# An attention kernel with a gated MLP: the first batch's maxima on the upper halves of float32 words, three weight blocks at the head of the load queue

## The chip, the cores and the metric

The kernel runs on one core of a Trainium2 chip. The metric is the time of one execution on the device in microseconds (us), as the median of several runs. The engines of the core work side by side, each through a list of its own: TensorE (PE, matrix products; its weight loads are shown as PEld), VectorE (DVE), ScalarE (ACT), GpSimd (POOL) and SyncE (SP), which here only issues DMAs.

## The reference, cut to what matters

Eight batches with eight heads of causal attention with a decay go into a two-layer MLP whose gate is `h * tanh(softplus(h))`. q, k and v are float32 with 576 rows of 64 per head; the MLP has 512 inputs, 2,048 hidden values and 512 outputs for 4,608 tokens.

```python
scores = scale * np.matmul(q, k.transpose(0, 1, 3, 2))
cum = np.cumsum(np.log(np.clip(f, 0.0001, 1.0)), axis=-1)
scores = np.where(causal, -1000000000.0, scores + cum[:, :, :, None] - cum[:, :, None, :])
scores = scores - np.max(scores, axis=-1, keepdims=True)
attn = np.exp(scores)
attn = attn / (np.sum(attn, axis=-1, keepdims=True) + 1e-09)
x = np.matmul(attn, v)            # all heads of a token side by side: 4608 x 512
h = x @ w_in
out = (h * np.tanh(np.log1p(np.exp(h)))) @ w_out
```

A row's maximum is only subtracted ahead of the exponential, and the division by the sum of the exponentials takes it out again. So it need not be exact.

## The kernel before

Two heads are worked on together as a pair, four pairs to a batch, 32 in all. Pairs 0 to 3 (the first batch, `g < NB`) go another way than the rest. A first pass, `max_items` (L1161), multiplies q with k on TensorE in float32, adds a row of decay sums (`rk`) and the causal mask, and VectorE reduces each block to row maxima (`mx`). The maxima are turned on TensorE (`mpad`, `mr`), and a second pass, `st_items`, makes the scores again, in float32 and transposed, with the maxima inside the product, so that their exponentials (`pt`) can go straight into the product with v. The maxima pass has diagonal blocks (`diag`, four of 128 columns for each of two heads), three wider ones (`t31` with 384 and 128, `t2` with 256 columns) and the last 64 rows of both heads on the full array (`t4a` with 512 columns, `t4b` with 64). Two heads' products of 64 rows run side by side in the two halves of the array.

Weights come in 32 blocks of 128 x 512 float32 values, as 64-bit words. `load_weights` (L882) brings one block by DMA; `convert_weights` (L888) makes from it, in three VectorE operations, words that ScalarE squares and sums (`junk<-wall`, into `wsq`); `scale_weights` adds the sums over the partitions on TensorE (`wsc<-wsq`, then `b<-wsc,ones`) and makes a factor from them; `split_weights` stores the scaled block as an upper half in f16 (VectorE or ScalarE) and the remainder in f16 (VectorE, `wall<-wall,wsc`). The first half of the blocks have places of their own; a later block goes to a place that a conversion has left.

`decay` (L782) makes the decay sums on VectorE and ScalarE and writes them to DRAM in two DMAs (`cumd`); `prep_first` reads rows of them back (`rk`). The write of the first head group carries the mark `rows0`. An operation with a gate counts as a reader of that mark, so it is put behind that write: all weight loads have the gate, and so have v's first loads.

The order of the work is not written out. A `Program` records all operations with their dependencies and ranks, and a planner (`schedule`, `forward`) sorts them into one list for each engine, by a model of their durations; some operations may go to either of two engines. Where the model sees TensorE idle in the first 140 us, it puts in fillers, products of `idm` and `idh` that nothing reads. An engine takes its list strictly in order. So a small edit moves rows far from itself.

In the program's lists, `qk_0`, `qk_1`, `hl` and part of `xa` are the four places that pairs 0 to 3 of q and k are loaded to, in this order; `b_0` with a number is a PSUM bank; `st_1` and `st_0` hold the decay sums while they are made.

Of the kernel before, what the change touches and what calls it, by code (L numbers as in the profile page):

```python
# [14 lines left out]
BF16 = mybir.dt.bfloat16  # L15
# [15 lines left out]
NP = 4  # L31
CH = 512
NF = 16
# [54 lines left out]
OFS = 0  # L88
KL0 = 100
KLS = 50  # L90
KS0 = 600
KSS = 50
KE0 = 900
# [7 lines left out]
NB = 4  # L101
# [580 lines left out]
def attn_moe(ctx: ExitStack, tc: tile.TileContext, qk, v, f, w_in, w_out, out):  # L682
# [99 lines left out]
    def decay():  # L782
        _, on, cm, r1 = tmp
        nc.vector.memset(on, 1.0)
        nc.vector.tensor_scalar(out=ft, in0=ft, scalar1=1e-4, scalar2=1.0, op0=ALU.max, op1=ALU.min)
        nc.scalar.activation(out=ft, in_=ft, func=AF.Ln)
        nc.scalar.preload_act_table_set("exp_and_others")
        nc.vector.tensor_tensor_scan(
            out=cm, data0=on, data1=ft, initial=0.0, op0=ALU.mult, op1=ALU.add)
        c = flat(ST2[1])[:, 0 : 3 * S].rearrange("p (r s) -> p r s", r=3)  # L790
        nc.vector.tensor_scalar(out=c[:, 0], in0=cm, scalar1=-8.0, scalar2=None, op0=ALU.mult)
        nc.vector.scalar_tensor_tensor(
            out=r1, in0=cm, scalar=-8.0, in1=c[:, 0], op0=ALU.mult, op1=ALU.subtract)
        nc.vector.tensor_copy(out=c[:, 1], in_=r1)
        nc.vector.tensor_tensor(out=c[:, 2], in0=r1, in1=c[:, 1], op=ALU.subtract)
        nc.mark = "sums"
        for h in (slice(0, H), slice(H, BH)):
            nc.mark = None if h.start else "sums"
            nc.sync.dma_start(out=cumd[h], in_=c[h])
        nc.mark = None  # L800
# [20 lines left out]
    def square_sum(o, x, scale=1.0):  # L821
        junk = sp.tile([P, S], BF16, name="junk", tag="junk", bufs=1)
        nc.scalar.activation(
            out=junk[:, 0 : free(x)] if len(x.shape) == 2 else junk.rearrange("p (n d) -> p n d", d=D),
            in_=x, func=AF.Square, scale=scale, accum_out=o)
# [41 lines left out]
    def step(x, j):  # L867
        return j + x * W1
# [12 lines left out]

    def load_weights(i):  # L882
        which, j = worder[i]
        nc.gate = 'rows0'
        nc.sync.dma_start(out=home[i], in_=(w_in, w_out)[which][:, j])
        nc.gate = None

    def convert_weights(i):  # L888

        x, j = worder[i]  # L890
        w = wall[:, i + 1].bitcast(F32)
        r, o = home[i], w.bitcast(I32)
        nc.vector.tensor_scalar(
            out=o, in0=r[:, 1::2], scalar1=3, scalar2=0x3FFFFFF8,
            op0=ALU.logical_shift_left, op1=ALU.bitwise_and)
        nc.vector.scalar_tensor_tensor(
            out=o, in0=r[:, 1::2], scalar=-(1 << 30), in1=o, op0=ALU.bitwise_and, op1=ALU.bitwise_or)
        nc.vector.scalar_tensor_tensor(
            out=o, in0=r[:, 0::2], scalar=29, in1=o, op0=ALU.logical_shift_right, op1=ALU.bitwise_or)
        square_sum(wsq[:, step(x, j), x : x + 1], w)  # L900

    def scale_weights(t0, t1):
# [146 lines left out]
        nbank += 1  # L1049
        return psum(nbank % 4)  # L1050

    def load_qk(g):
        b, p = divmod(g, NP)
        if g == 2:
            t = sp.tile([P, 2, S], F32, name=f"qk{g}", tag="hl", bufs=NHL)
        elif g == 3:
            t = xa[1].rearrange("p a h n -> p (a h n)").bitcast(F32)[:, 0 : 2 * S]
            t = t.rearrange("p (t s) -> p t s", t=2)
        else:
            t = sp.tile([P, 2, S], F32, name=f"qk{g}", tag="qk32", bufs=NQK)  # L1060
        nc.sync.dma_start(out=t, in_=qk[b, p])
        st[g]["qk"] = t

    def place1(g):
        return (g - NB) % 2

    def qz(g):
        return spare1[:, g * P : (g + 1) * P]
# [91 lines left out]

    def max_items(g):  # L1161

        x, k, z, s = st[g]["qk"], rk[:, g], qz(g), st[g]

        def begin():

# [563 lines left out]
    def gated_by(gate, f):  # L1730
        nc.gate = gate
        f()
        nc.gate = None
# [10 lines left out]
        out=psum(RB)[:, 0:DN], lhsT=idh, rhs=idm.unsqueeze(1).to_broadcast([P, DN // P, P]), start=True, stop=True))]  # L1744
    NG = B * NP
    nc.sync.dma_start(out=ft, in_=f)
    load_qk(0)
    decay()
    load_qk(1)
    for g in (2, 3):  # L1750
        gated_by('rows0', lambda: load_qk(g))

    A = []
    marks = {}
# [2 lines left out]
    def a0(fn, g=NG):  # L1757
        A.extend(leading(g, [(fn, 0)]))
# [4 lines left out]
    def slot(t, what=("max", "st", "pv")):  # L1763

        groups = []
        ahead = "max" in what and t < NG
        if ahead:
            groups.append(leading(t, max_items(t)) if t < NB else [])
        if "st" in what and 0 <= t - 1 < NG:
            groups.append(leading(t - 1, (st_items if t - 1 < NB else new_st_items)(t - 1)))  # L1770
        if "pv" in what and 0 <= t - 2 < NG:
            groups.append(leading(t - 2, (pv_items if t - 2 < NB else new_pv_items)(t - 2) + x_items(t - 2)))
        if ahead:
            b, p = divmod(t, NP)
            b1 = (t - 9 + NV) // NP
            if t == NP * b1 + 9 - NV and b1 < B - 1:
                a0(lambda: amax_v(b1 + 1))
            if t == 0 or t == EX:
                a0(lambda: prep(t), t)
                a0(lambda: prep2(t), t)  # L1780
        if ahead and t == LV0:
            a0(lambda: gated_by('rows0', lambda: load_v(0)), 0)
            a0(lambda: amax_v(0), 0)
            a0(lambda: scale_chunk2(0))
        if "st" in what and 0 <= t - 1 < NG:
            a0(lambda: prep_v(t - 1), t - 1)
            b, p = divmod(t - 1, NP)
            if p == 7 - NV and b + 1 < B:
                a0(lambda: gated_by('rows2' if b == 0 else None, lambda: load_v(b + 1)))
        merged = sorted(  # L1790
            ((k + 0.5) / len(x) * (0.75 if ahead and gi == 0 else 1.0), gi, k)
            for gi, x in enumerate(groups) for k in range(len(x)))
        half_done = not ahead
        for fr, gi, k in merged:
            A.append(groups[gi][k] + ((t, gi, k),))
            if not half_done and fr > 0.35:
                half_done = True
                if t + 1 < NB and t + 1 != EX:
                    a0(lambda: prep(t + 1), t + 1)
                elif t >= NB:  # L1800
                    a0(lambda: prep(t))
                if 4 <= t + 2 <= NB:
                    a0(lambda: load_qk(t + 2))
                elif NB < t + 1 < NG:
                    a0(lambda: load_qk(t + 1))
        if ahead and t + 1 < NB and t + 1 != EX:
            a0(lambda: prep2(t + 1), t + 1)
        elif ahead and t >= NB:
            a0(lambda: prep2(t))
        if "pv" in what and 0 <= t - 2 < NG:  # L1810
            marks[t - 2] = len(A)
# [72 lines left out]


    first = marks[NP - 1]
    wq = [ranked([KL0 + k * KLS, 0, 0.1], lambda i=k: load_weights(i)) for k in range(NF)]
    for t0, t1 in zip([0] + TB, TB):
        now = [place[x, t - x * W1] for t in range(t0, t1) for x in range(2) if 0 <= t - x * W1 < NF]
        for i in now:  # L1890
# [93 lines left out]
```

## Time and profile before

| | us |
|---|---|
| median of 3 runs | 1023.21 |
| lowest and highest | 1021.28, 1026.99 |
| the profiled execution | 1025.73 |
| span of the profiled execution, first to last instruction | 1023.6 |

| engine | busy us | share of the span | instructions |
|---|---|---|---|
| TensorE | 989.9 | 97% | 7838 |
| VectorE | 737.2 | 72% | 2018 |
| ScalarE | 712.4 | 70% | 1350 |
| GpSimd | 16.1 | 2% | 79 |

The mean granted clock of TensorE is 0.992 of full speed. A matrix product's end is modelled, so products overlap in the records: the distance from one start to the next tells what one costs, and a busy share of 97% is not 97% of what the array could do. Nearly all instructions are recorded by one helper line (L331), so rows are told apart by the names of what they write and read: `out<-in`.

### The profile page before, as it was taken

How to read it: one execution, taken by the hardware profiler on the slowest of the kernel's cores; microseconds unless marked ns; L12 is line 12 of the kernel's file. 1: busy time of each engine (PE TensorE's matmuls, PEld its weight loads, DVE VectorE, ACT ScalarE, POOL GpSimd, SP SyncE). 2: the span in 40 equal slices, each digit the busy share in tenths (PEclk: the TensorE clock that was granted, in tenths of full speed). 3: DMA queues.
4: the chain of work that ended last, by engine and by line, in shares of the span. 5: the costliest groups of instructions: out<-in, count | busy, mean ns of one | idle time of the engine just before them, and what ended most of it. 6: DMA issues, size and time to landing. Idle time of an engine off the chain costs nothing.

```text
span 1023.6 us, 20891 instructions
## 1 busy us (share of the span) xinstructions
PE 989.9 (97%) x7838; PEld 547.7 (54%) x7838; DVE 737.2 (72%) x2018; ACT 712.4 (70%) x1350; POOL 16.1 (2%) x79
## 2 busy tenths in 40 slices
PE   5999999999999999999999999999999999999998
PEld 4687444444555555445454555454545555656664
DVE  5999899997777677666767767676777659952432
ACT  2567899979777877777777777888777664533323
POOL 4000000000000000000000000000000000000000
PEclk9899899999999999999999999999999999999999
DMA  6968856678867767686868776777666343001001
GB/s 200 377 222 210 177 131 128 134 155 181 175 137 167 173 137 156 133 177 137 158 137 189 140 154 144 146 156 136 130 134 134 68 78 73 4 1 43 1 1 42
DMA packets 265079, 137.50 MB, mean 134 GB/s; under 512 B 237522, under 2 KB 237714, under 8 KB 264978
## 3 DMA queue, kind: packets, MB, share of 16 engines
q1 hardware_dynamic: 264978, 136.17, 59.3%
q8 instruction: 61, 1.00, 0.4%
q14 instruction: 40, 0.33, 0.1%
HBM read 45.46 MB, written 9.66 MB: 54 GB/s over the span
## 4 chain that ended last, share of the span: by engine, by line
PE 66%; DVE 17%; DMA 7%; ACT 5%; issue 3%; SPq 1%; POOL 1%; ACTq 0%; DVEq 0%; POOLq 0%
PE b L331 66%; DVE wall L331 4%; DVE b L331 3%; DMA pt<-hb 2%; DMA st<-hl 2%; DVE hb L331 2%; SPq L331 1%; DMA qk<-in_qk_dram 1%; DVE hl L331 1%; DMA wall<-in_w_out_dram 1%; ACT junk L331 1%; DVE x L331 1%; DVE gl L331 1%; ACT rk L331 1%; ACT more_e L331 1%
## 5 line engine op out<-in xcount | busy, mean ns | idle before, releaser
L331 PEld LDWEIGHTS <-wall 128*128 128x128 f16 x3372 | 323.1, 98 | 360.7 <-issue 25.2
L331 PE MATMUL b<-gh,wall 128*128 128x512 f16 x1152 | 366.1, 379 | 0.3 <-DVE wsc L331 0.3
L331 PE MATMUL b<-xa,wall 128*128 128x512 f16 (+1 forms) x1602 | 346.1, 366 | 8.9 <-ACT me L331 4.4
L331 PE MATMUL b<-gl,wall 128*128 128x512 f16 x576 | 218.3, 379 | 0.0
L331 DVE SCALAR_TENSOR_TENSOR gl<-me,gsc,gh 128x512 f16<-128x512 f32 x144 | 106.6, 751 | 33.5 <-ACT gh L331 32.4
L331 ACT ACTIVATE me<-b,cinv 128x512 f32<-128x512 f32 (+1 forms) x130 | 85.2, 660 | 53.9 <-PE b L331 52.7
L331 DVE CUSTOM_DVE_ANT_0 b<-b,mskw 128x256 f32<-128x256 f32 (+2 forms) x168 | 95.3, 570 | 21.3 <-PE b L331 17.0
L331 PE MATMUL b<-st 128*128 128x384 f16 (+11 forms) x672 | 106.8, 299 | 2.6 <-ACT rk L331 1.3
L331 ACT ACT_TABLE_LOAD x76 | 97.5, 1283 | 1.3
L331 PEld LDWEIGHTS <-st 67*128 67x128 f16 (+3 forms) x864 | 68.9, 101 | 54.4 <-issue 16.9
L331 PE MATMUL b<-vv,pt 128*128 128x65 f16 (+3 forms) x2464 | 94.4, 199 | 3.5 <-DVE x L331 1.6
L331 ACT ACTIVATE more_e<-b,mn 128x512 f32<-128x512 f32 (+3 forms) x126 | 64.9, 543 | 37.5 <-DVE mn L331 33.5
L331 PEld LDWEIGHTS <-pt 128*128 128x128 f16 (+1 forms) x2352 | 72.4, 101 | 19.2 <-DMA pt<-hb 3.5
L331 ACT ACTIVATE rk<-b,mn 128x512 f32<-128x512 f32 (+3 forms) x126 | 64.4, 543 | 24.2 <-DVE mn L331 22.7
L331 DVE TENSOR_TENSOR hb<-more_e,hb 128x512 f16<-128x512 f32 x84 | 57.7, 688 | 28.3 <-ACT hb L331 27.8
L331 DVE TENSOR_TENSOR hb<-rk,hb 128x512 f16<-128x512 f32 x84 | 57.4, 688 | 22.7 <-ACT hb L331 22.4
L331 DVE TENSOR_SCALAR gh<-me,gsc 128x512 f16<-128x512 f32 x67 | 32.4, 485 | 41.6 <-ACT me L331 40.4
L331 ACT ACTIVATE hb<-more_e 128x512 f16<-128x512 f32 x84 | 51.9, 626 | 7.1 <-DMA pt<-hb 6.6
L331 ACT ACTIVATE gh<-me,gsc 128x512 f16<-128x512 f32 x77 | 54.9, 718 | 1.7
L331 DVE TENSOR_TENSOR me<-b,hb 128x256 f32<-128x256 f32 x42 | 18.0, 432 | 51.1 <-PE b L331 50.5
L331 ACT ACTIVATE hb<-rk 128x512 f16<-128x512 f32 x84 | 51.4, 625 | 4.2 <-DMA pt<-hb 2.3
L331 ACT ACTIVATE junk<-qk 128x576 bf16<-128x576 f32 x56 | 38.1, 680 | 19.7 <-DMA qk<-in_qk_dram 19.0
(189 smaller groups left out, 1078.8 us busy)
## 6 DMA issues: line engine op xcount, KB each, us to landing
st<-hl SPq DMA_DIRECT2D x168, 144.0 KB
qk<-in_qk_dram SPq DMA_DIRECT2D x30, 576.0 KB
out_dram<-ot SPq DMA_DIRECT2D x36, 256.0 KB
v<-in_v_dram SPq DMA_DIRECT2D x30, 288.0 KB
wall<-in_w_in_dram SPq DMA_DIRECT2D x16, 512.0 KB
wall<-in_w_out_dram SPq DMA_DIRECT2D x16, 512.0 KB
pt<-hb SPq DMA_TRANSPOSE x168
hl<-in_qk_dram SPq DMA_DIRECT2D x1, 576.0 KB
```

Source lines behind the costliest of these rows:

```text
L331: r = getattr(real[eng], method)(*a, **kw)
```

## The change

In `max_items` the views of q, k and the copied tail `z` become bf16 views of every second 16-bit element, which are the upper halves of the float32 words. The products there become 16-bit products, with the values cut to their upper halves; the second pass is as it was. `NUG = 3` weight blocks lose the gate `rows0`, so that their loads may go ahead of the write of the decay sums, and their conversions get a gate of their own, `parts`, which is set by the last VectorE operation of the decay sums. They are recorded right behind pair 0's load. Pairs 2 and 3 of q and k, before recorded at the head, are now recorded behind pair 0's preparation.

```diff
+NUG = 3
@@ decay
+        nc.mark = "parts"
         nc.vector.tensor_tensor(out=c[:, 2], in0=r1, in1=c[:, 1], op=ALU.subtract)
@@ load_weights
-        nc.gate = 'rows0'
+        nc.gate = 'rows0' if i >= NUG else None
         nc.sync.dma_start(out=home[i], in_=(w_in, w_out)[which][:, j])
@@ convert_weights
+        nc.gate = "parts" if i < NUG else None
         nc.vector.tensor_scalar(
...
+        nc.gate = None
         square_sum(wsq[:, step(x, j), x : x + 1], w)
@@ load_qk, now place_qk for the tile and load_qk for the DMA
+        if "qk" not in st[g]:
+            place_qk(g)
+        nc.sync.dma_start(out=st[g]["qk"], in_=qk[g // NP, g % NP])
@@ max_items
-        x, k, z, s = st[g]["qk"], rk[:, g], qz(g), st[g]
+        k, s = rk[:, g], st[g]
+        x = st[g]["qk"].bitcast(BF16)[:, :, 1::2]
+        z = qz(g).bitcast(BF16)[:, 1::2]
@@ the head of the program
+    for g in range(NB):
+        place_qk(g)
     load_qk(0)
+    for k in range(NUG):
+        load_weights(k)
     decay()
     load_qk(1)
-    for g in (2, 3):
-        gated_by('rows0', lambda: load_qk(g))
@@ slot
+        if ahead and t == 0:
+            for g in (2, 3):
+                a0(lambda g=g: gated_by('rows0', lambda: load_qk(g)), 0)
@@ the weights' queue
-    wq = [ranked([KL0 + k * KLS, 0, 0.1], lambda i=k: load_weights(i)) for k in range(NF)]
+    wq = [ranked([KL0 + k * KLS, 0, 0.1], lambda i=k: load_weights(i)) for k in range(NUG, NF)]
```

How the planner's lists change is shown at three places. The first is the head of SyncE's list. Before:

```order
L331 DMA st_1_87<-in_f_dram 64x576
L331 DMA hl_110<-in_qk_dram 128x1152
L331 DMA xa_90<-in_qk_dram 128x1152
L331 DMA qk_0_108<-in_qk_dram 128x1152
L331 DMA qk_1_109<-in_qk_dram 128x1152
L331 DMA cumd<-st_1_87 8x1728
...
L331 DMA vv_114<-in_v_dram 128x9x64
L331 DMA wall<-in_w_in_dram 128x1024 x4
L331 DMA wall<-in_w_out_dram 128x1024
```

The same place after:

```order
L332 DMA st_1_87<-in_f_dram 64x576
L332 DMA qk_0_108<-in_qk_dram 128x1152
L332 DMA wall<-in_w_in_dram 128x1024 x3
L332 DMA qk_1_109<-in_qk_dram 128x1152
L332 DMA cumd<-st_1_87 8x1728
...
L332 DMA vv_114<-in_v_dram 128x9x64
L332 DMA wall<-in_w_in_dram 128x1024
L332 DMA hl_110<-in_qk_dram 128x1152
L332 DMA wall<-in_w_out_dram 128x1024
```

Pair 0 has gone to the front with three weight blocks behind it; the loads of pairs 2 (`hl`) and 3 (`xa`, eight loads further on) have gone behind v and the fourth weight block.

The second place is VectorE's list from the last operation of the decay sums to the first reductions. Before:

```order
L331 TENSOR_TENSOR st_1_87<-st_0_86,st_1_87 64x576
L331 TENSOR_REDUCE mx_119<-b_0_124 128x1
L331 TENSOR_REDUCE mx_119<-b_0_125 128x1
L331 TENSOR_REDUCE mx_119<-b_0_120 128x4
...
L331 TENSOR_REDUCE mx_127<-b_0_124 128x4
L331 TENSOR_REDUCE am_m_117<-vc_115 128x1
L331 TENSOR_SCALAR am_m_117<-am_m_117 128x1
L331 TENSOR_SCALAR wall<-wall 128x512
```

After:

```order
L332 TENSOR_TENSOR st_1_87<-st_0_86,st_1_87 64x576
L332 TENSOR_SCALAR wall<-wall 128x512 x2
L332 SCALAR_TENSOR_TENSOR wall<-wall 128x512 x4
L332 TENSOR_SCALAR wall<-wall 128x512
...
L332 SCALAR_TENSOR_TENSOR wsc<-b_0_107,wba 128x4
L332 TENSOR_SCALAR wsc<-wsc 128x4
L332 TENSOR_SCALAR wiv<-wsc 128x4
L332 SCALAR_TENSOR_TENSOR wall<-wall,wsc 128x512
L332 TENSOR_REDUCE mx_119<-b_0_120 128x4
```

Three conversions, the scaling of two blocks and one remainder now stand between the sums and the first reduction; a second remainder stands among the reductions. `am_m<-vc`, the sum of v's squares, and the fourth block come after the reductions, as the first block did.

The third place is TensorE's list behind the first, unfinished products of pair 0. Before:

```order
L331 MATMUL b_0_122<-qk_0_108 128x384
L331 MATMUL b_0_123<-qk_0_108 128x384
L331 LDWEIGHTS idh
L331 MATMUL b_0_107<-idm,idh 128x128
...
L331 MATMUL b_0_120<-rk,xa_90 128x128
L331 LDWEIGHTS xa_90
L331 MATMUL b_0_121<-rk,xa_90 128x128
```

After:

```order
L332 LDWEIGHTS qk_0_108
L332 MATMUL b_0_123<-qk_0_108 128x384
L332 LDWEIGHTS idh
L332 MATMUL b_0_107<-idm,idh 128x128
...
L332 MATMUL b_0_107<-wsc,ones 128x4
L332 LDWEIGHTS idh
L332 MATMUL b_0_107<-idm,idh 128x128
...
L332 MATMUL b_0_120<-rk,xa_90 128x128
```

Where 34 fillers stood, there are 82 and then, behind the first column sum of weights (`wsc,ones`), 5 more. A 16-bit product has one product row and a weight load of its own. In the whole program there are 148 fillers in place of 78. The late parts of the lists are the same in both, row for row: the last 1,155 rows of VectorE's, the last 338 of SyncE's.

## Rows read from the trace of the kernel before

**Rows 1.** The page, part 4: shares of the chain of work that ended last.

```profile
PE 66%; DVE 17%; DMA 7%; ACT 5%; issue 3%; SPq 1%; POOL 1%; ACTq 0%; DVEq 0%; POOLq 0%
```

**Rows 2.** Stretches, us: busy of PE, PEld, DVE, ACT, POOL; PE's clock; DMA share; GB/s.

```profile
10.00:26.00 16.00, 11.43 (x140) 8.62 (x136) 5.52 (x15) 3.10 (x8) 2.59 (x13) 0.95 0.70 173
26.00:40.00 14.00, 12.46 (x111) 7.99 (x112) 13.33 (x40) 8.18 (x23) 0.41 (x2) 0.81 1.03 402
40.00:80.00 40.00, 39.70 (x511) 33.05 (x509) 39.61 (x105) 26.82 (x68) 0.00 (x0) 1.00 0.71 242
...
97.00:112.00 15.00, 14.96 (x73) 10.32 (x74) 12.39 (x35) 11.62 (x29) 0.14 (x1) 0.66 0.73 149
...
140.00:220.00 80.00, 78.43 (x611) 39.48 (x609) 79.36 (x237) 77.01 (x133) 0.97 (x3) 1.00 0.62 130
...
260.00:860.00 600.00, 595.08 (x4717) 303.64 (x4715) 422.11 (x1174) 451.46 (x856) 2.91 (x21) 1.00 0.68 141
```

**Rows 3.** Timeline, DVE: start, us, instruction, count, [idle before and what ended it].

```profile
8.88 0.75 DVE L331 TENSOR_TENSOR st<-st,st 64x576 f16<-64x576 f32 x1
15.40 0.76 DVE L331 TENSOR_REDUCE mx<-b 128x1 f32<-128x256 f32 x2 [5.77 <-PE b L331]
...
23.82 0.16 DVE L331 TENSOR_REDUCE am_m<-vc 128x1 f32<-128x4 f32 x1 [2.61 <-ACT junk L331]
...
25.58 0.43 DVE L331 TENSOR_SCALAR wall<-wall 128x512 int32<-128x512 int32 x1 [1.42 <-DMA wall<-in_w_in_dram]
...
31.20 0.18 DVE L331 TENSOR_SCALAR mpad<-mx 128x18 f16<-128x18 f32 x1
...
94.39 0.43 DVE L331 TENSOR_SCALAR wall<-wall 128x512 int32<-128x512 int32 x1 [1.99 <-DMA wall<-in_w_out_dram]
```

**Rows 4.** Timeline, SP's queue.

```profile
9.72 0.70 SPq L331 DMA_DIRECT2D cumd<-st  x2
...
19.65 2.63 SPq L331 DMA_DIRECT2D wall<-in_w_in_dram  x4
```

**Rows 5.** Timeline, PE's products, from 15 to 106 us.

```profile
15.03 0.34 PE L331 MATMUL b<-rk,xa 64*128 64x128 f16 x4
...
19.30 1.10 PE L331 MATMUL b<-qk,xa 128*128 128x512 f32 x2
20.24 0.38 PE L331 MATMUL b<-rk,xa 128*128 128x512 f16 x1
...
24.21 0.38 PE L331 MATMUL b<-am_m,ones 128*128 128x1 f32 x2 [3.15 <-DVE am_m L331]
26.73 2.08 PE L331 MATMUL b<-qk,xa 128*128 128x512 f32 x2 [2.13 <-DVE cols L331]
...
97.04 3.29 PE L331 MATMUL b<-vv,pt 128*128 128x65 f32 x26 [1.64 <-DVE x L331]
...
105.18 2.72 PE L331 MATMUL b<-xa,wall 128*128 128x512 f16 x6
```

**Rows 6.** Groups by form, DVE, 0 to 260 us: count | busy us, mean ns.

```profile
L331 DVE SCALAR_TENSOR_TENSOR wall<-wall 128x512 int32<-128x512 int32 x64 | 43.3, 687 | 0.2
L331 DVE SCALAR_TENSOR_TENSOR wall<-wall,wsc 128x512 f16<-128x512 f32 x32 | 23.9, 747 | 0.0
...
L331 DVE TENSOR_SCALAR wall<-wall 128x512 int32<-128x512 int32 x32 | 13.3, 423 | 3.4 <-DMA wall<-in_w_out_dram 2.0 <-DMA wall<-in_w_in_dram 1.4
```

**Rows 7.** Timeline, PE, second score pass of pair 3: 32-bit and 16-bit products.

```profile
87.46 0.81 PE L331 MATMUL b<-xa 64*128 64x384 f32 x4
88.11 0.19 PE L331 MATMUL b<-idm,msk 64*128 64x64 f16 x1
...
88.33 0.33 PE L331 MATMUL b<-xa,rk 64*128 64x384 f16 x2
88.50 0.39 PE L331 MATMUL b<-xa 64*128 64x128 f32 x4
```

**Rows 8.** The chain in order of time, one piece: start, us, what.

```profile
84.88 9.48 DMA wall<-in_w_out_dram
```

More of the change, by code (lines that the diff above doesn't have):

```diff
@@ L1050, in score_bank, with place_qk @@
         return psum(nbank % 4)
-    def load_qk(g):
-        b, p = divmod(g, NP)
+    def place_qk(g):
         if g == 2:
@@ L1060, in load_qk @@
             t = sp.tile([P, 2, S], F32, name=f"qk{g}", tag="qk32", bufs=NQK)
-        nc.sync.dma_start(out=t, in_=qk[b, p])
         st[g]["qk"] = t
+    def load_qk(g):
+        if "qk" not in st[g]:
+            place_qk(g)
+        nc.sync.dma_start(out=st[g]["qk"], in_=qk[g // NP, g % NP])
     def place1(g):
```

## The prediction

> **What bounds the kernel now.** I read the chain of work that ended last, then the table of stretches, then the timelines of VectorE, TensorE and SyncE's queue over the first 110 us. The chain is TensorE's for 66% and VectorE's for 17% [rows 1]. The table says where each has its part [rows 2]: from 260 to 860 us TensorE is busy for 595 of 600 us and VectorE for 422, so that is TensorE's stretch, and nothing there can start earlier unless what stands ahead of it does. From 140 to 220 us VectorE (79.4 of 80) and ScalarE (77.0) are full and TensorE is close behind. From 40 to 80 us TensorE (39.7) and VectorE (39.6) are full together. The only long holes are at the start: from 10 to 26 us VectorE works 5.5 us of 16, from 26 to 40 us TensorE's granted clock is 0.81 on average, and from 97 to 112 us it is 0.66.
>
> The change touches only work of the first 100 us, and the diff of the orders bears this out: the last 1,155 of VectorE's about 2,010 rows, and the last 338 of SyncE's 601, stand in the same sequence before and after. So the question is by how much the first batch (pairs 0 to 3) ends earlier, and how much of that arrives at the common tail.
>
> What holds VectorE at the start is in its timeline [rows 3]. The decay sums end at 9.63 us (8.88 + 0.75). Then it waits 5.77 us for the first finished maxima, because each score product ends with a row of the sums that has been through DRAM: SyncE sends them at 9.72 [rows 4], TensorE gets the first at 15.03 [rows 5]. It waits 2.61 us for ScalarE's squares of v and 1.42 us for the first weight block, which SyncE sends out only at 19.65, behind all of that [rows 4]. Adding the 0.5 us pieces between, 10.5 us of VectorE's time in this window are empty [rows 2].
>
> **Part 1: three weight blocks early.** A block's conversion is one shift (13.3 us for 32, 0.42 each) and two combinations (43.3 us for 64, 0.68 each), so 1.77 us [rows 6]; in a row they overlap a little, and I take 1.6. Three blocks are 4.8 us. The order shows them right behind the last operation of the decay sums, with the scaling of the first two blocks (about 0.4 us of small operations) and two of their remainders (23.9 us for 32, 0.75 each, so 1.5) ahead of or among the first reductions. That is 6.7 us of VectorE's work which before lay behind 25.6 us. It lies in the 5.77 us wait, so the first reductions, before at 15.40, start about 1.8 us later: 9.63, plus 4.8 of conversion, about 0.3 until ScalarE has squared the second block, 0.6 for the column sum on TensorE, 0.4 of scaling, 0.6 until ScalarE has the upper half, 0.75 for the remainder, is 17.1. The seven or so reductions that were spread over 15.4 to 21.2 us at TensorE's pace then run without a pause and, with the second remainder among them, end at about 22.3; the next thing, the sum of v's squares, was ready at 23.82 [rows 3]. So the delay is covered with 1.5 us to spare. The fourth block is SyncE's first weight load behind v, where the first was: it lands at about the same 25.6 us. VectorE is then 6.7 us of work ahead, and its holes from 9.6 to 25.6 us have shrunk from 10.5 to about 4.
>
> What the early loads may cost: at the head of the queue 1.5 MB of weights take the place of 1.15 MB of pairs 2 and 3, a little over 0.3 MB more. The loads of before were done by then, since nothing of SyncE's waits at 9.72; a further 0.3 MB or so at the 402 GB/s of the stretch from 26 to 40 us [rows 2] is under 1 us, and the sums are written only at 9.72. I take nothing, with 1 us as the other end. Pair 0 is first in the queue now, so its load is off the path.
>
> Pairs 2 and 3 are now loaded behind the fourth and between later blocks. Pair 2's products stand behind pair 0's second score pass, so a load sent at about 20 us has time. But blocks five to nine then stand behind 1.15 MB more, while VectorE comes to them 6.7 us sooner. At 402 GB/s [rows 2] those bytes are 2.9 us. I put the waits for blocks between 30 and 40 us at 0 to 3 us and take 1, since the common conversion pace there (1.6 us a block and other work between) is slower than a block's 1.3 us of transfer.
>
> **Part 2: maxima on 16-bit halves.** The price of a 32-bit product against a 16-bit one is in one stretch where both run on the same shapes, two heads side by side [rows 7]: 384 columns in 32 bits take from 87.46 to 88.11, 0.65 us; in 16 bits from 88.33 to 88.50, 0.17. That is 1.25 ns a column. On the full array, 512 columns in 32 bits take from 19.30 to 20.24, 0.94 us [rows 5]; by the 16-bit rate (0.44 ns a column) 0.23, so 1.4 ns a column saved. A pair's maxima have 1,280 columns of the first kind (diagonal blocks 512, t31 512, t2 256) and 576 of the second (t4a, t4b): 1.6 + 0.8 = 2.4 us a pair, 9.6 us for four. No row shows TensorE reading every second 16-bit element; so the bounds are the 16-bit price (2.4 us saved) and, if such a read went at the 32-bit rate, nothing. I take the 16-bit price, since the other records of that stretch run at it whatever their tile.
>
> [...]
>
> Of the 9.6 us, pair 0's and most of pair 1's lie in time when TensorE waits or runs fillers. One piece of pair 0's is on the path: t4a starts at 26.73, behind the 3.15 and the following wait that took TensorE's clock to half, and takes 2.08 us [rows 5]; VectorE has the maxima ready only at 31.20 [rows 3]. After the change the same product takes about 0.5, and the reductions stand closer: the maxima are ready at about 28.9. That is 2.3 us on the path to pair 0's second score pass. Pairs 2 and 3 lie inside the 40 us in which TensorE is full [rows 2]: 2 x 2.4 = 4.8 us. Together 7.1 us for TensorE until the first batch ends.
>
> **The sum.** TensorE's path to the end of the first batch shrinks by 7.1 us, VectorE's list there by 6.7 us plus what the planner hands to ScalarE (in the whole program five upper halves of blocks fewer on VectorE, which I set against the 1 us of waits for blocks). Both engines are full from 40 to 80 us, so the smaller gain counts: 7 us, rounded. ScalarE is a third idle there [rows 2] and covers its part. From 97 us on everything is as before, only earlier, until the two orders meet, and from there it is TensorE's. I carry the 7 us through. The profiled execution took 1025.73 us with a span of 1023.6; less 7 it is 1018.7. It lies 2.5 us above the median of 1023.21, and by that scale I forecast **1016 us**, with a range of its own of 1013 to 1020.
>
> **The rivals.**
> *More: the half-clock stretch goes too.* At 94.39 VectorE had stood 1.99 us for a weight block; the chain shows that load under way for 9.48 us [rows 8]. TensorE, which waited behind it for 1.64 us, went on at 97.04 [rows 5], and from there to 112 us its clock is 0.66 [rows 2]. In the new order late conversions stand further back there (the 25th block's is some 100 rows later), so the block may be there in time. The wait (2 us) and half of what 15 us at 0.66 lose (5 us, half of it beside the wait for the first batch's transposes) make 4 to 5 us more: 1011.
> *Less: the lead is given back.* From 112 to 220 us VectorE and ScalarE are full and do the same work as before; if first-batch results come earlier but the weights' scale factors or the loads behind converted blocks do not, VectorE meets DMA waits later instead of early, and of 7 us some 2 arrive: 1021.
> *Slower: TensorE's clock.* With 32-bit products gone, TensorE is no longer full from 40 to 80 us and waits for VectorE instead; the order has no fillers on TensorE once pair 0's second score pass is under way. Waits of 3.15 and 1.64 us came ahead of the two slow stretches [rows 5]. [...] Against it: VectorE gains about as much as TensorE, so TensorE's waits should be short ones. [...]
> *It doesn't do what it says:* if the strided read were as slow as 32 bits, TensorE, full from 40 to 80 us, would be as late as before, and part 1 would bring only what TensorE waits for VectorE up to 40 us, 1 to 2 us: 1022. I count it with *less*.
>
> **How the numbers follow.** The forecast has 0.48, more 0.17, less 0.24, slower 0.11. A measurement of this kernel tells about 0.5%, 5.1 us, from no change: faster means under 1018.1, slower over 1028.3. Of the forecast's case about an eighth lies above 1018.1. So faster is 0.42 + 0.17 = 0.59, same 0.06 + 0.23 = 0.29, and slower 0.12. The range from 1008 to 1023 holds forecast, more and nearly all of less, and leaves out slower.
>
> **What would show it.** Right: conversions at 9.7 us on VectorE, reductions from about 17, maxima of pair 0 ready near 29 and not 31.2, t4a's two records become one of under 0.6 us, the first product of x and weights at about 98 in place of 105.18 [rows 5], and the stretch from 260 us on of unchanged length. Wrong: 16-bit products at over 0.3 us for 384 columns; VectorE waiting for weights for over 3 us between 26 and 45 us; a granted clock under 1 between 40 and 80 us; or a first batch that ends 7 us sooner with chunk 0 ending where it did.

## The result

The changed kernel takes 1015.76 us (median of 6 runs, 1011.01 to 1017.22) against 1023.7 us before (6 runs); the ratio is 0.9912 with a 95% interval of [0.9883, 0.9941]. The forecast was 1016. The profiled execution has a span of 1015.0 us where before had 1023.6.

| | before | after |
|---|---|---|
| span, us | 1023.6 | 1015.0 |
| TensorE busy | 989.9 | 981.7 |
| VectorE busy | 737.2 | 737.3 |
| ScalarE busy | 712.4 | 711.2 |
| mean granted clock | 0.992 | 0.990 |

The shares of the chain of work that ended last, and the stretches that answer to [rows 1, 2] (columns as there):

```profile
PE 70%; DVE 12%; ACT 8%; DMA 5%; issue 3%; SPq 1%; ACTq 0%; DVEq 0%
```

```profile
10.00:26.00 16.00, 11.27 (x172) 9.40 (x170) 13.10 (x33) 6.71 (x16) 5.13 (x12) 0.89 0.76 205
26.00:40.00 14.00, 13.30 (x166) 10.43 (x165) 12.77 (x38) 10.04 (x26) 2.20 (x6) 0.88 1.03 409
40.00:80.00 40.00, 39.12 (x473) 30.90 (x472) 36.85 (x104) 26.07 (x64) 0.00 (x0) 0.91 0.73 233
97.00:112.00 15.00, 9.45 (x66) 4.38 (x65) 14.26 (x47) 13.61 (x30) 0.00 (x0) 0.88 0.88 186
140.00:220.00 80.00, 76.86 (x584) 38.54 (x583) 77.41 (x233) 72.43 (x131) 0.42 (x3) 1.00 0.70 144
260.00:860.00 600.00, 594.32 (x4712) 305.11 (x4711) 424.71 (x1179) 451.23 (x852) 2.93 (x21) 1.00 0.67 139
```

VectorE's hole from 10 to 26 us is 2.9 us where it was 10.5, and the long middle is as full of TensorE as it was. New is the third row: between 40 and 80 us the granted clock is 0.91, and VectorE, full before, has 3.15 us of holes in this execution (0.45 us in another, e1 below). VectorE's timeline at the start answers to [rows 3]:

```profile
9.10 0.75 DVE L332 TENSOR_TENSOR st<-st,st 64x576 f16<-64x576 f32 x1
9.77 1.15 DVE L332 TENSOR_SCALAR wall<-wall 128x512 int32<-128x512 int32 x2
10.85 2.48 DVE L332 SCALAR_TENSOR_TENSOR wall<-wall 128x512 int32<-128x512 int32 x4
...
17.96 3.40 DVE L332 TENSOR_REDUCE mx<-b 128x4 f32<-128x512 f32 x9 [0.28 <-PE b L332]
...
21.94 1.28 DVE L332 TENSOR_REDUCE mx<-b 128x4 f32<-128x512 f32 x2
23.92 0.16 DVE L332 TENSOR_REDUCE am_m<-vc 128x1 f32<-128x4 f32 x1 [0.70 <-ACT junk L332]
...
24.91 0.43 DVE L332 TENSOR_SCALAR wall<-wall 128x512 int32<-128x512 int32 x1 [0.64 <-DMA wall<-in_w_in_dram]
...
28.31 0.18 DVE L332 TENSOR_SCALAR mpad<-mx 128x18 f16<-128x18 f32 x1
```

The conversions stand in the old wait, the first reductions come at 17.96 instead of 15.40, and pair 0's maxima are ready at 28.31 instead of 31.20. TensorE's timeline answers to [rows 5, 7]:

```profile
22.67 0.39 PE L332 MATMUL b<-qk,xa 128*128 128x512 bf16 x1 [0.41 <-DVE mx L332]
...
26.05 0.39 PE L332 MATMUL b<-qk,xa 128*128 128x512 bf16 x1 [0.82 <-DVE cols L332]
...
38.91 2.25 PE L332 MATMUL b<-v,pt 128*128 128x65 f32 x16 [0.54 <-ACT pt L332]
...
66.04 0.34 PE L332 MATMUL b<-xa 64*128 64x384 bf16 x2
66.22 0.32 PE L332 MATMUL b<-rk,xa 64*128 64x384 f16 x2
...
68.17 0.39 PE L332 MATMUL b<-xa 128*128 128x512 bf16 x1
68.40 0.38 PE L332 MATMUL b<-rk,xa 128*128 128x512 f16 x1
...
95.90 3.18 PE L332 MATMUL b<-xa,wall 128*128 128x512 f16 x14
...
103.01 0.25 PE L332 MATMUL b<-vv,pt 128*128 128x65 f16 x3 [2.37 <-ACT rk L332]
...
109.68 0.58 PE L332 MATMUL b<-xa,wall 128*128 128x512 f16 x1 [2.70 <-ACT me L332]
```

The first product of x and weights starts at 95.90, before at 105.18. Behind it TensorE stands for 2.37 and 2.70 us. Of the 9.3 us won there 8.6 are left at the end.

**TensorE's books.** Since TensorE ends the program (its products lead the chain to 1011.25 of 1015.0 us), its span can be split into four parts: idle (span less busy time), what the half clock cost (span times one less the mean clock; idle time at the half clock is counted in it too), fillers (busy time of `b<-idm,idh`), and the rest, which is useful work. The rows for the changed kernel are these, the page's part 1 and the group of fillers (count, busy us, mean ns):

```profile
PE 981.7 (97%) x7844; PEld 542.2 (53%) x7844; DVE 737.3 (73%) x2010; ACT 711.2 (70%) x1354; POOL 19.9 (2%) x79
```

```profile
L332 PE MATMUL b<-idm,idh 128*128 128x128 f16 x148 | 13.0, 251 | 0.3 <-DVE wsc L332 0.3
```

So 1015.0 - 981.7 = 33.3 idle, 1015.0 x 0.010 = 10.2 for the clock, 13.0 of fillers, and 981.7 - 10.2 - 13.0 = 958.5 of work. The same for every kernel of the study (ends are modelled and some fillers ran at the half clock (0.50 from 28 to 30 us in the kernel before, with 16 of them from 29.02), so a difference of 2 us says nothing: the same program gives 958.5 and 960.3 of work); the last two columns are medians and ratios to the kernel before with their intervals:

| kernel | span | idle | clock | fillers | work | median, us | ratio |
|---|---|---|---|---|---|---|---|
| before | 1023.6 | 33.7 | 8.2 | 8.4 | 973.3 | 1023.7 | |
| after | 1015.0 | 33.3 | 10.2 | 13.0 | 958.5 | 1015.8 | 0.9912 [0.9883, 0.9941] |
| e1 after, again | 1010.5 | 32.1 | 5.1 | 13.0 | 960.3 | 1015.1 | 0.9911 [0.9887, 0.9934] |
| e2 new order, f32 | 1021.6 | 27.9 | 8.2 | 11.8 | 973.7 | 1021.2 | 0.9970 [0.9953, 0.9986] |
| e3 old order, 16 bits | 1026.3 | 45.1 | 13.3 | 9.4 | 958.5 | 1029.4 | 1.0063 [1.0041, 1.0086] |
| e4 after, one wait filled | 1009.9 | 31.6 | 3.0 | 14.3 | 961.0 | 1013.1 | 0.9898 [0.9870, 0.9926] |
| e5 after, six waits filled | 1008.9 | 26.6 | 0.0 | 20.8 | 961.5 | 1010.5 | 0.9866 [0.9840, 0.9892] |
| e6 old order, 16 bits, filled | 1021.3 | 36.2 | 2.0 | 19.3 | 963.8 | 1025.9 | 1.0014 [0.9993, 1.0034] |
| e7 16 bits alone, planned | 1012.2 | 33.7 | 5.1 | 12.7 | 960.7 | 1013.4 | 0.9892 [0.9869, 0.9915] |
| e8 loads alone, planned | 1025.7 | 36.7 | 12.3 | 5.6 | 971.1 | 1027.3 | 1.0019 [1.0000, 1.0039] |
| e9 no early block | 1022.9 | 32.9 | 20.5 | 12.3 | 957.2 | 1014.8 | 0.9927 [0.9899, 0.9955] |
| e10 six early blocks | 1017.7 | 32.8 | 10.2 | 16.1 | 958.6 | 1019.3 | 0.9944 [0.9923, 0.9965] |
| e11 e7, filled | 1011.3 | 27.6 | 0.0 | 20.7 | 963.0 | 1013.6 | 0.9897 [0.9873, 0.9921] |
| e12 e9, filled | 1012.6 | 26.9 | 2.0 | 21.1 | 962.6 | 1014.0 | 0.9904 [0.9884, 0.9925] |

After against before: 14.8 us less work, 4.6 us more fillers, 2.0 us more for the clock, 0.4 less idle; together 8.6. The profile of e9 is not typical of its runs (its clock is 0.980, that of seven of the twelve 0.990 to 0.993), so its row stands for that one execution.

### The profile page after: what moved, and what is told of

Read it like the earlier page. It is cut to its first block, busy times and chain, and to the rows that moved or that the text cites. A ratio compares the mean times of both kernels' runs of the same rounds, so it can differ in the third digit from the quotient of the medians.

```text
span 1015.0 us, 20882 instructions
## 1 busy us (share of the span) xinstructions
PE 981.7 (97%) x7844; PEld 542.2 (53%) x7844; DVE 737.3 (73%) x2010; ACT 711.2 (70%) x1354; POOL 19.9 (2%) x79
## 4 chain that ended last, share of the span: by engine, by line
PE 70%; DVE 12%; ACT 8%; DMA 5%; issue 3%; SPq 1%; ACTq 0%; DVEq 0%
PE b L332 70%; DVE wall L332 2%; DVE b L332 2%; DMA pt<-hb 2%; DMA qk<-in_qk_dram 2%; ACT junk L332 1%; ACT L332 1%; ACT hb L332 1%; SPq L332 1%; DVE hb L332 1%; ACT rk L332 1%; ACT more_e L332 1%; ACT me L332 1%; DVE st L332 1%; DMA wall<-in_w_in_dram 1%
## 5 line engine op out<-in xcount | busy, mean ns | idle before, releaser
L332 DVE SCALAR_TENSOR_TENSOR gl<-me,gsc,gh 128x512 f16<-128x512 f32 x144 | 106.1, 747 | 33.7 <-ACT gh L332 32.8
L332 DVE CUSTOM_DVE_ANT_0 b<-b,mskw 128x256 f32<-128x256 f32 (+2 forms) x168 | 94.7, 568 | 20.1 <-PE b L332 17.1
L332 PE MATMUL b<-st 128*64 128x64 f16 (+11 forms) x672 | 106.0, 298 | 2.8 <-ACT more_e L332 0.8
L332 ACT ACTIVATE more_e<-b,mn 128x512 f32<-128x512 f32 (+3 forms) x126 | 65.0, 544 | 36.2 <-DVE mn L332 33.6
L332 ACT ACTIVATE junk<-qk 128x576 bf16<-128x576 f32 x56 | 38.1, 680 | 26.1 <-DMA qk<-in_qk_dram 25.6
```

The lines of the kernel that those rows point to most:

```text
L332: r = getattr(real[eng], method)(*a, **kw)
```

## The experiments

### One price at a time, in the order of either kernel

The planner sorts everything anew after any edit, so a part that is undone in the source changes all lists. To keep a list and change only what its products cost, the planner was shown one type and the program was given the other. In e2 the plan is the changed kernel's and the products are float32; in e3 the plan is that of the kernel before and the products are 16-bit. Every engine's sequence is row for row that of the kernel it comes from.

```diff
+        def twin(shown, run):
+            nc.twin[id(shown)] = run
+            return shown
...
-                r = getattr(real[eng], method)(*a, **kw)
+                r = getattr(real[eng], method)(*a, **{n: self.twin.get(id(x), x) for n, x in kw.items()})
```

**e1.**

> The changed kernel itself, unaltered, as the mate of the next three on the same chip. Expected: 1015.8 us median, as measured, ratio to the kernel before 0.991, and the same slow-clock stretches of TensorE in the profile (at 16, 27, 40 to 47 and 108 to 115 us).

Measured 1015.1 us, as expected, but the profile is another: the clock is 1.00 from 40 to 80 us, and TensorE's slow stretches lie elsewhere.

```profile
40.00:80.00 40.00, 39.11 (x514) 31.41 (x514) 39.55 (x112) 28.32 (x68) 0.14 (x1) 1.00 0.77 247
97.00:112.00 15.00, 10.37 (x63) 5.15 (x64) 12.15 (x39) 12.54 (x25) 0.00 (x0) 0.77 0.75 148
```

So the same program has its slow stretches at other places in other executions. Over the twelve of the changed kernel the mean clock goes from 0.997 (1011.0 us) to 0.988 (1017.1 us): between these two executions 9 us of lost full-speed time go with 6 us of the end. In between the tie is loose: the five executions at 0.993 take 1014.1 to 1017.2 us.

**e2.**

> The changed kernel's lists of instructions, every engine's in the changed kernel's own sequence (planned with 16-bit costs), but the maxima products read q and k as float32 again. Only the price of the products is undone. Theory of the prediction: TensorE is full from 40 to 80 us, so pairs 2 and 3 bring back 4.8 us and pair 0's piece on the path 2.3: 1021 to 1023. Rival (the early blocks and the order carry the gain, the products ran in TensorE's spare time): 1016 to 1018.

Measured 1021.2 us: the products are worth 6.1 us in the new order, between the 4.8 and 7.1 that the theory had. The rival falls. What is left to the order and the loads is 2 to 3 us. With the longer products it is VectorE that waits in this order:

```profile
40.00:80.00 40.00, 40.00 (x430) 31.79 (x431) 30.03 (x87) 18.64 (x46) 0.00 (x0) 0.88 0.58 195
```

TensorE has no gap there, and VectorE works for 30.03 us of 40.

**e3.**

> The lists of the kernel before, in its own sequence with its own loads (planned with float32 costs), but the maxima products read the upper halves. Only the price of the products is changed. Theory of the prediction: VectorE's list is as long as before and full from 40 to 80 us, so only pair 0's 2.3 us arrive: 1021 to 1022 (ratio 0.998). Rival (the products alone bring it all, VectorE has slack): 1015 to 1018.

Measured 1029.4 us, slower than before by 0.6% with the interval clear of one. Both theories missed. The stretches from 26 us on, a wait of TensorE and one of VectorE:

```profile
26.00:40.00 14.00, 11.80 (x112) 7.86 (x112) 12.89 (x38) 8.18 (x23) 0.41 (x2) 0.59 1.03 406
40.00:80.00 40.00, 35.51 (x478) 29.20 (x477) 39.86 (x107) 27.85 (x71) 0.00 (x0) 1.00 0.72 246
82.00:91.50 9.50, 9.50 (x59) 7.03 (x60) 8.60 (x22) 4.88 (x12) 0.00 (x0) 0.50 0.97 274
```

```profile
79.65 3.58 PE L332 MATMUL b<-vv,pt 128*128 128x65 f32 x25 [1.17 <-DVE mx L332]
```

```profile
95.26 0.70 DVE L332 CUSTOM_DVE_ANT_0 b<-b,mskw 128x512 f32<-128x512 f32 x1 [3.88 <-PE b L332]
```

VectorE is as full as before (39.86 of 40), so the shorter products turn into waits of TensorE (35.51 busy where it was 39.70). Behind them the clock falls, from 82 on TensorE runs at half of it, and VectorE stands for 3.88 us. In the books: 14.8 us less work, 11.4 more idle, 5.1 more for the clock. This is the mechanism of the prediction's slower rival, in an order that was planned for longer products; but the idle time takes back most of what was saved before the clock turns it into a loss, and the clock is low ahead of the stretch from 40 to 80 us (0.59 from 26 to 40 us) and behind it, not in it.

### Is it the clock?

In e4, e5 and e6 filler products (128 columns, read by nothing) are put ahead of waits of TensorE, at fixed places of the list and in a PSUM bank that is free there. Nothing else moves.

```diff
+        more, seen = {92: (7, 32), 194: (7, 14), 204: (7, 12), 338: (7, 10), 855: (4, 38), 899: (4, 40)}, 0
         for i, o in order:
+            if i < 0 or ops[i][0][o][0] == "tensor":
+                for k in range(more.get(seen, (0, 0))[1]):
+                    real["tensor"].matmul(**dict(self.warm[1][0][3], out=self.free_bank(more[seen][0])))
+                seen += 1 if i < 0 else sum(x[1] in ("matmul", "transpose") for x in ops[i][0][o][1])
```

The numbers are: place in TensorE's list, bank, count. In e4 only the place 338 is filled; e6 has eight places of the old order.

**e4.**

> The changed kernel in its own sequence, with ten filler products (128 columns each, about 0.55 us together, their result is read by nothing) put on TensorE right ahead of the 0.54 us wait at 38.4 us, behind which the clock fell to 0.50 from 40.3 to 47.1 us. If that small wait brought the clock down and TensorE's time there is on the path: clock 1.00 from 40 to 47, and 3.4 us less, 1012 to 1013. Rival A (the clock falls all the same, for what lay ahead of the wait): 1016. Rival B (the clock stays up, but VectorE sets the end of the first batch): clock 1.00 and 1015 to 1016.

Measured 1013.1 us, an interval that overlaps e1's. The profile has the small wait filled and the clock at 1.00:

```profile
36.00:40.00 4.00, 4.00 (x44) 3.73 (x42) 3.90 (x12) 3.38 (x7) 0.34 (x1) 1.00 1.03 410
40.00:80.00 40.00, 39.12 (x512) 31.46 (x512) 39.56 (x111) 28.02 (x67) 0.14 (x1) 1.00 0.78 251
```

But e1 has 1.00 there without it. That this one wait of 0.54 us brings the clock down is not shown.

**e5.**

> The changed kernel in its own sequence with 146 filler products of 128 columns (read by nothing) ahead of six waits of TensorE: 32 at 13 us, 14 at 23.3, 12 at 25.2, 10 at 38.4, and 38 and 40 at 100.6 and 107.0, the last two into a PSUM bank that is free there. Theory (what is left of TensorE's slow clock follows its waits, and the last two stretches, from 40 and from 99 or 108 us, lie on the path): all executions at a mean granted clock of 0.997 or more, the median at the fastest of the changed kernel, 1010 to 1012. Rival (the waits end with VectorE and ScalarE, so a full clock between them buys nothing): 1014 to 1016.

Measured 1010.5 us, five of six executions at a clock of 1.000 and one at 0.998 (1009.4 to 1013.1 us). This is the theory, and the fastest kernel of the study: 1.3% under the kernel before. The rival falls: a full clock is worth some 5 us here (1010.5 us against e1's 1015.1 at 0.988 to 0.995). (The intervals of the two ratios, e1's and e5's, still meet at 0.989; of the twelve unfilled executions one, at a clock of 0.997, is as short as 1011.0 us.)

**e6.**

> The kernel before in its own sequence with 16-bit maxima products, as in the run that was 6 us slower than before, and in it 182 filler products ahead of eight waits of TensorE: 76 at 19.3 us, 20 at 24.5, 20 at 28.6, 12 at 32.1, 6 at 42.7, 20 at 49.4, 8 at 54.8 and 20 at 78.5. Theory (the 6 us were TensorE's clock, which fell because the shorter products leave it waiting for VectorE): clock back at 0.993 or more and the time back to 1021 to 1024. Rival (the loss has another cause: the order does not fit the shorter products): 1027 to 1030 with the clock restored.

Measured 1025.9 us beside 1025.5 us of the kernel before on that chip: ratio 1.0014, against 1.0063 unfilled, and the intervals don't meet. The time lies between the two expectations and the clock is 0.990 to 1.000 (0.980 to 0.987 in e3), so the ratio has to decide: most of the loss of e3 was the clock. And with the clock held, the products bring nothing in the old order. VectorE is busy there for 39.89 of the 40 us from 40 to 80, and pair 3's maxima are ready at 80.40 us, hardly sooner than before (81.76).

### One part at a time, planned anew

**e7.** `max_items` of the changed kernel in the kernel before; everything else as before: its edit is the three lines in `max_items` alone.

> The kernel before with the 16-bit maxima alone, its loads as they were, planned anew: the planner sees the shorter products and puts 133 fillers in place of 78. The late part of the order differs from both kernels. Theory (VectorE's list is what limits, the products bring little, but the planner's fillers hold the clock): 1020 to 1024. Rival (the products alone are worth most of the 8 us once the planner knows of them): 1014 to 1017. Rival (the clock falls as in the old order): 1027 to 1031.

Measured 1013.4 us: the products alone bring all of it, once the planner knows of them. The hole at the start is as wide as before and the gain is there all the same:

```profile
10.00:26.00 16.00, 11.43 (x167) 9.50 (x164) 4.94 (x14) 3.10 (x8) 3.62 (x16) 0.92 0.72 180
...
40.00:80.00 40.00, 38.99 (x475) 32.04 (x476) 39.29 (x120) 30.89 (x76) 0.14 (x1) 1.00 0.80 256
```

Where VectorE's time comes from is seen in its list ahead of the last pair's finished maxima (`mpad<-mx` of pair 3). Of the shifts that begin a conversion (`wall<-wall`, TENSOR_SCALAR) 23 stand there in the kernel before and in e3, 14 in e7 and 17 in the changed kernel. The row itself, in the kernel before, e3, e7 and the changed kernel:

```profile
81.76 0.18 DVE L331 TENSOR_SCALAR mpad<-mx 128x18 f16<-128x18 f32 x1
```

```profile
80.74 0.21 DVE L332 TENSOR_SCALAR mpad<-mx 128x18 f16<-128x18 f32 x1
```

```profile
64.71 0.17 DVE L331 TENSOR_SCALAR mpad<-mx 128x18 f16<-128x18 f32 x1
```

```profile
71.75 0.17 DVE L332 TENSOR_SCALAR mpad<-mx 128x18 f16<-128x18 f32 x1
```

The planner puts nine conversions, 9 x 1.77 = 15.9 us of VectorE, behind the first batch's maxima, and these are ready 17 us sooner. By 97 us six fewer have begun than before (21 against 27; 23 in the changed kernel), while six more remainders (0.75 us each) have begun; by 180 us all 32 conversions have begun. That the gain comes from the place of the conversions, and not from another difference of the two lists, was not run by itself.

**e8.** The same three lines the other way: the changed kernel with float32 maxima.

> The changed kernel with the maxima products in float32 again and planned so: three early blocks and the moved loads alone. The late part of the order differs from both kernels. Theory (VectorE is ahead but TensorE is then full to the end of the first batch): 1019 to 1022. Rival (the lead of 6.7 us arrives): 1015 to 1017. Rival (the moved loads of pairs 2 and 3 cost): 1024 or more.

Measured 1027.3 us, against 1025.5 us of the kernel before on that chip (1.0019, [1.0000, 1.0039]). The first two expectations missed; the time is that of the third, 1024 or more, though by the ratio it is hardly slower than before. The early blocks and the moved loads without the shorter products gain nothing in this plan, and TensorE's books show 3.0 us more idle and 4.1 more for the clock. That the moved loads cost it is not borne out: from 10 to 140 us VectorE waits for a load once, 1.4 us for a weight block, and TensorE not at all for q and k. The plan has 77 fillers, not 148, all twelve executions have a clock of 0.984 to 0.990, and the clock is low where the hole had been:

```profile
26.00:40.00 14.00, 10.69 (x53) 6.01 (x55) 11.03 (x34) 5.26 (x15) 1.04 (x5) 0.55 1.02 404
```

With its waits filled e8 was not run, so what the clock takes there is open. Part of the loss may also be the late order, which is another in e7 and e8 than in either kernel.

**e9.** The changed kernel with `NUG = 0`: its late order is the changed kernel's.

```diff
-NUG = 3
+NUG = 0
```

> The changed kernel with NUG = 0: 16-bit maxima and the moved loads of pairs 2 and 3, but no weight block ahead of the decay sums, planned anew. The late part of the order is the changed kernel's (the last 1,233 operations of VectorE). Theory of the prediction (the 6.7 us that VectorE gains at the start are needed for the gain): 1019 to 1022. Rival, from the run with the 16-bit maxima alone (TensorE's shorter list is the gain, the early blocks fill a hole that nobody waits for): 1012 to 1016, as the changed kernel.

The median of 12 executions is 1014.8 us, the changed kernel's. So the theory that the early lead is needed falls in this form too. But the executions spread from 1012.8 to 1027.4 us with clocks from 0.993 to 0.980.

**e10.** `NUG = 6`.

> The changed kernel with NUG = 6: six early blocks in place of three, planned anew. Theory of the prediction (a lead of VectorE is worth time as far as the hole goes; six blocks are 10 us of conversion in a wait of 5.8, so the first reductions come some 4 us later): 1016 to 1020. Rival (the early blocks are worth nothing either way as long as TensorE's list stays the same): 1013 to 1016.

Measured 1019.3 us. Pair 0's maxima are ready at 33.1 us in place of 28.3, and the first product of x and weights comes at 99.5: what goes beyond the hole delays the first batch. The time is the theory's and outside the rival's range; the interval of the ratio still overlaps the changed kernel's.

**e11, e12.** e7 and e9 with their waits filled, as in e5.

> The run with the 16-bit maxima alone (loads as before), in its own sequence, with 130 filler products ahead of five waits of TensorE: 58 at 20.5 us, 20 at 25.2, 8 at 35.3, 10 at 71.6 and 34 at 98.4. Both this and the changed kernel with its filled waits then run at a full clock, so that the early blocks are compared without the clock. If the early blocks bring nothing: clock 0.999 and 1009 to 1011, as the changed kernel filled (1010.5). If they bring their lead: 1013 or more.

> The run without early blocks (NUG = 0, pairs 2 and 3 moved) in its own sequence, with 164 filler products ahead of six waits of TensorE: 24 at 12.8 us, 50 at 20.9, 20 at 33.3, and 30, 24 and 16 at about 100 to 120 us into a PSUM bank that is free there. Its late order is the changed kernel's, and the clock is meant to be full in both, so against the changed kernel with its waits filled (1010.5) this is the three early blocks without the clock. If they bring nothing: 1009.5 to 1011.5. If VectorE's lead is worth something once the clock is out of the way: 1013 or more. With the fillers the wide spread (1012.8 to 1027.4, clocks down to 0.98) should go: all executions within 4 us.

Measured 1013.6 and 1014.0 us at clocks of 0.999 to 1.000 and 0.995 to 0.998. The spread of e9 is gone (1013.5 to 1014.4 us in four executions). The full clock brought e11 nothing: e7, the same order without the fillers, took 1013.4 us at 0.994 to 0.997. So what the clock gives back depends on the order. Against e5's 1010.5 both are some 3.5 us longer, as the early blocks' lead would have it. The stretches of e5 and then of e12:

```profile
80.00:112.00 32.00, 30.52 (x326) 21.69 (x321) 30.66 (x98) 29.86 (x67) 0.14 (x1) 1.00 0.98 176
112.00:220.00 108.00, 103.31 (x788) 51.87 (x787) 104.38 (x305) 98.89 (x174) 0.57 (x4) 1.00 0.77 172
```

```profile
80.00:112.00 32.00, 27.77 (x306) 20.87 (x300) 31.48 (x97) 28.24 (x65) 0.14 (x1) 0.95 0.91 215
112.00:220.00 108.00, 104.68 (x792) 52.35 (x791) 106.87 (x314) 101.76 (x183) 0.55 (x4) 1.00 0.75 164
```

e12 has the old waits at the start again:

```profile
15.73 4.60 DVE L337 TENSOR_REDUCE mx<-b 128x4 f32<-128x512 f32 x11 [5.78 <-PE b L337]
23.45 0.16 DVE L337 TENSOR_REDUCE am_m<-vc 128x1 f32<-128x4 f32 x1 [3.12 <-ACT junk L337]
25.03 0.43 DVE L337 TENSOR_SCALAR wall<-wall 128x512 int32<-128x512 int32 x1 [1.24 <-DMA wall<-in_w_in_dram]
```

Yet pair 0's maxima are ready at 28.4 us in e12 and at 28.0 in e5. The difference comes later: VectorE has 0.8 us more to do from 80 to 112 us and 2.5 us more from 112 to 220, with 1.1 us of that stretch empty against 3.6 in e5. Of the 3.7 us by which the two profiled spans differ, 2.0 are the clock's in the books, since e12's is not quite full (0.95 from 80 to 112 us). The kernels are planned apart and were timed beside different runs of the kernel before (1025.5 us for e5, 1024.7 for e11, 1022.9 for e12), and the intervals of the ratios overlap, though only one of e5's six executions is as long as the shortest of e11 and e12. So a lead of up to 3.5 us is likely and its size is not shown.

## Why the prediction was right or wrong

**The time** is right, 1015.76 against 1016, and so is the sign. The working behind it is right in its prices, but one step of the sum is wrong. That the sum comes within 1 us of the gain all the same is in part luck: the products were priced too low, the second part was not needed as the sum has it, and the profiled execution lost 2 us more to the clock than before.

**Part 1, the start.** Right, to within a microsecond: conversions at 9.77 us, reductions from 17.96 (17.1 was worked out), done at 23.2 (22.3), the fourth block at 24.91 (25.6), and 2.9 us of holes left (about 4). The margin ahead of v's sum was 0.70 us and not 1.5. No load made VectorE wait between 25 and 130 us; 1 us had been taken for it. (The mark `rows0` is set in the program by the reads of pair 0's rows in `prep_first`, which stand behind the write; a gated load is behind both.)

**Part 2, the price.** Right. At full clock (1.00 from 66 to 69 us) the 384 columns take from 66.04 to 66.22, 0.18 us, and 512 on the full array from 68.17 to 68.40, 0.23 us, as the 0.17 us for 384 columns in [rows 7] and the 0.23 us worked out for 512. So here every second 16-bit element is read at the price of contiguous ones, 0.18 us against 0.17. The sum was a little small: 9.6 us of TensorE's work for four pairs were worked out, and the books give 971 to 974 us of work in the three float32 kernels and 957 to 964 in the eleven 16-bit ones, some 12 us. Pair 0's piece, put at 2.3 us, measures 2.9.

**The sum: the step that failed** is "both engines are full from 40 to 80 us, so the smaller gain counts". It takes VectorE's list up to the end of the first batch as a fixed amount of work that only the early blocks can shorten. It is not: conversions fill it, and a plan that knows TensorE to be ready sooner puts some of them behind the first batch: 14 stand ahead of pair 3's maxima in e7, and 23 before. The prediction saw such a move (in *More*, the 25th block's conversion some 100 rows later) and left it out of the sum. e7 has no early block, VectorE's full hole, and the whole gain. Where the lists are held still, the step is right, and e3 and e6 show it: VectorE full, nothing arrives. So of the 7 us the text credits two parts that must meet, while the runs show one that suffices (the products, if planned) and a second that may add up to 3.5 us with the clock held, and nothing that can be seen without. Nor does that lead show in the first batch's maxima: pair 3's are ready at 68.66 us in e5 and at 67.44 in e12. It shows from there on: the first product of x and weights comes at 92.81 us against 95.62, and VectorE has less to do from 80 to 220 us.

**The rivals.** *Slower* names what the runs show, waits of TensorE and a slow clock behind them (in e3 a wait of 1.17 us to 79.65 and 0.50 from 82), but one such stretch does not take back the gain. In the profiled execution the clock did fall between 40 and 80 us, which the prediction had among the signs of being wrong; in e1 it did not:

```profile
36.00:40.00 4.00, 3.46 (x45) 3.28 (x42) 3.86 (x11) 3.67 (x9) 0.83 (x2) 1.00 1.04 412
40.50:46.50 6.00, 6.00 (x66) 4.04 (x65) 4.83 (x11) 2.71 (x8) 0.00 (x0) 0.50 0.98 388
48.00:52.00 4.00, 4.00 (x44) 3.01 (x43) 2.34 (x8) 1.50 (x4) 0.00 (x0) 1.00 0.16 26
```

The wait ahead of it is 0.54 us, and the price is about 3 us for these 6 us at a clock of 0.50, less than half of the 7.9 us gained. (The order does have one filler later than the text says, at 45.38 us.) What one such wait costs by itself no run shows (e4, with this one filled, takes 1013.1 us, and its interval overlaps e1's), so the 0.11 for this rival was the author's estimate. It was wrong to seek its effect only in the changed order: e3, the products without the new plan, is where it decides, and there the clock is worth some 5 us (e3 against e6). *More*: the load that VectorE stood for at 94.39 is gone, but TensorE waits for ScalarE instead (2.37 and 2.70 us), and the clock in 97 to 112 us is 0.88 in one execution and 0.77 in the other. *Less* did not happen: 9.3 us at the first product of x and weights, 8.6 at the end. Its reading that VectorE and ScalarE are full from 112 us on holds from 140; from 112 to 140 us they are busy for 25.63 and 25.27 of 28 us before. That the strided read is slow is excluded by its rows (0.18 us for 384 columns).

**What would be the next step** is in e5: the changed kernel with six waits of TensorE filled takes 1010.5 us.

Open: whether any single wait brings the clock down (e4 can't tell); how much of e8's loss is the clock or the late order; and how much two plans of nearly the same program can differ in time. Each variant of e7 to e10 was planned once. That the products gain without the early blocks is seen in two plans (e7 and e9); the few microseconds of the early blocks lie between plans and may be the plans'.

## What to carry to other kernels

When a planner or a list decides the order, price a cheaper operation with the plan that it will get: the same products cost 0.6% in the old order and gained 1.1% in a plan made for them. Look then at which other work the plan moves. Split the bound engine's span into idle, clock, fillers and work before and after: work that is saved and comes back as idle or as a slower clock is seen at once. Where TensorE waits on the path in short pieces, products that nobody reads can be worth their place (some 5 us in e5 and e6, nothing in e11), and a kernel whose time varies from one execution to the next may be varying with its clock (e9: 1012.8 us at 0.993, 1027.4 us at 0.980).

## What the runs showed of the hardware that was not expected

In e9's profiled execution the granted clock is 0.50 throughout these 23.5 us, in which TensorE is busy all the time:

```profile
36.50:60.00 23.50, 23.50 (x173) 18.70 (x169) 11.17 (x32) 9.22 (x25) 0.00 (x0) 0.50 0.49 184
```

Ahead of it TensorE had been idle for 1.27 us, to 34.54. What it ran in the stretch are mostly float32 products of 65 columns (some 12 us by their starts) and products of 64 rows. The slow stretch before [rows 5], behind the wait at 97.04 (the clock is 0.81 from 99 to 100 us and 0.50 from 100 to 101), begins with float32 products of 65 columns too. That work of TensorE is enough to hold the clock up fits e5, with its waits filled and a clock of 1.000; it does not fit this stretch: an engine that the profile has as busy stayed at 0.50 for 23.5 us, and its records are as slow as that (the 512 columns of bf16 at 56.66 us take 0.40 us to the next start, in the changed kernel at 68.17 us and full clock 0.23). Why is open. And where the slow stretches of one and the same program lie differs between executions, as e1 shows beside the first profile (from 40 to 80 us 1.00 against 0.91).
